# A decode kernel whose query weights arrive in another order: the last 128 rows of w_q first, in four loads over two queues, into a V buffer that is still free

## The chip, the cores and the metric

The kernel runs on one core of one Trainium2 chip. The metric is the device time in microseconds (us), lower is better. The kernel before takes 203.89 us (median of 3 runs, 203.78 to 204.10).

Engines are named as the profile names them: PE is TensorE's matmul, PEld its weight load, DVE is VectorE, ACT is ScalarE, POOL is GpSimd, and SP is SyncE, which here only issues DMAs. A DMA is issued on the queue of the engine that issues it (q1 is SP's, q10 is ACT's) and is carried by 16 DMA engines.

## The reference, cut to what matters

One token goes through an attention block with a cache of 4096 positions and then a gated feed-forward block. All tensors are bf16.

```python
# x [1,1,640]; k_cache, v_cache [1,32,4096,128]; wq [640,4096]; wo [4096,640]
# w_gate, w_up [640,1728]; w_down [1728,640]
q = layernorm(x) @ wq                              # 32 heads of 128
scores = einsum("bhqd,bhkd->bhqk", q, k) * 128**-0.5
o = einsum("bhqk,bhkd->bhqd", softmax(scores), v)
h = x + o @ wo
n = layernorm(h)
out = h + (gelu(n @ w_gate) * (n @ w_up)) @ w_down
```

K and V are 32 MB each, w_q and w_o 5 MB each, the three feed-forward weights 2.1 MB each.

## The kernel before, in words

**Groups.** The 32 heads are worked in 8 groups of 4 (`HG`, `NG`). A group's K is one 4096 KB load into one of two buffers `kbuf`, its V one load into one of two buffers `vbuf`; a partition holds 128 positions of one head, 32 partitions make a head.

**Query.** `query(g)` (L314) makes the queries of one group: five matmuls (L318), one per chunk of 128 rows of w_q, with the normalised x repeated over 128 columns (`xb`) as the stationary operand, so that every partition gets the query; four ACT copies (L324) then put each head's part into `qb`. `wq_sb` lies in `arena`, 5 rows of w_q (40 KB) in each partition; the same arena later takes `wo_sb`. All queries go through one PSUM tile, `pq`.

**Scores.** DVE multiplies K with `qb` in four pieces a group (`mult`, L339, into three `prod` buffers), PE adds up over the 128 columns with matmuls by the identity (`fold`, L359 and L350), DVE reduces the rest (`red`, L366). `top`, `turn`, `head` and `soft` find the maximum and make the exponentials `P4` on ACT (L395). The last `mult` of a group frees its K buffer (`kfree`).

**Values.** PE multiplies P with V (`values`, L406), 32 matmuls a group in four parts; the last frees the V buffer (`vfree`). `extract`, `column`, `total`, `spread`, `gather` and `place` bring the result into the column form that `project` (L612, w_o) needs. The last group's values go another way (`values_last`, L414).

**Behind the attention.** Layernorm of h, `up` (L659) for w_gate and w_up, the gelu on 14 columns, `down` (L697) with w_down, a copy and the store.

**Order.** The order is written out by hand: each engine runs its instructions in the order in which the calls to `S.op` and `S.dma` stand, and `Sched` adds semaphore waits where a call names a token. All loads but x are on SP's queue, in program order, so an issue that waits holds up those behind it: w_q (L247), K0, K1 (L257), V0 (L266); then at the end of each step n of the main loop the next V and K, K with a wait for `kfree`, V with a wait for `vfree` (V1 has none). `load_wo` waits for the last query (`t_qlast`), since w_o takes w_q's place. x (L278) is on ACT's queue. In the main loop queries 0 and 1 stand ahead of step 0, and query n+1 stands in step n for n from 1.

**Start.** While w_q arrives, DVE and POOL make constants, PE turns x into columns (L302: five matmuls of one row), and `layernorm` (L281) makes `xb` (L297).

## Time and profile before

| | |
|---|---|
| median of 3 runs | 203.89 us |
| the profiled execution | 203.82 us |
| its span, first to last instruction | 202.6 us |
| PE busy | 153.4 us (76%) |
| DVE busy | 116.1 us (57%) |
| ACT busy | 30.5 us (15%) |
| POOL busy | 2.4 us (1%) |
| bytes read from HBM | 84.23 MB, 416 GB/s over the span |
| w_q, issue to landing | 15.3 us |
| K loads, issue to landing, median | 25.1 us |
| V loads, issue to landing, median | 23.2 us |

Spans and windows count from the span's start. "DMA share" is the mean busy share of the 16 DMA engines; in a short window it can be above 1, because a packet is counted, with its whole duration, where it starts. A wait is put down to what the profile saw end last. The chain of waits is followed back from the last instruction, at each step to what released it.

### The profile page before, as it was taken

The page shows a single profiled execution, that of the slowest core. Times are in us where ns is not written, and L with a number is a line of the kernel's source. Part 1 is how long each engine was busy: PE and PEld are TensorE (multiplying, and loading weights), DVE is VectorE, ACT ScalarE, POOL GpSimd, SP SyncE. Part 2 cuts the span into 40 slices and gives each one's busy share as a digit, 9 for nine tenths or more (in the row PEclk, how much of TensorE's full clock was granted, in tenths as well). Part 3 has the DMA queues.
Part 4 walks back from the last instruction along what each step waited for, and adds up shares of the span by engine and source line. Part 5 has one row for each costly group of instructions (what it writes and reads, how often), then busy time and mean ns, then how long its engine had stood idle before and what let it go on. Part 6 is the DMA issues. An engine that isn't in the chain of part 4 may idle for free.

```text
span 202.6 us, 2291 instructions
## 1 busy us (share of the span) xinstructions
PE 153.4 (76%) x1084; PEld 49.8 (25%) x860; DVE 116.1 (57%) x153; ACT 30.5 (15%) x110; POOL 2.4 (1%) x8
## 2 busy tenths in 40 slices
PE   1005348689969957999899399959777999977775
PEld 1001000002211220322122113212100244666572
DVE  6200087998199518883993499269999513301121
ACT  2002200006004200150060006000604004000000
POOL 1000000000000000000000000000000000200000
PEclk9999999999999996999999999999999999975555
DMA  7999999999999999999999999999999999989992
GB/s 251 412 469 414 414 434 453 459 414 414 421 450 427 459 409 414 440 429 440 443 421 414 434 440 440 434 427 411 440 427 446 385 427 457 450 382 438 423 396 102
DMA packets 3939, 84.37 MB, mean 416 GB/s; under 512 B 441, under 2 KB 570, under 8 KB 986
## 3 DMA queue, kind: packets, MB, share of 16 engines
q1 hardware_dynamic: 3928, 84.23, 97.4%
q8 instruction: 7, 0.11, 0.2%
q14 instruction: 2, 0.02, 0.0%
q10 hardware_dynamic: 2, 0.00, 0.0%
HBM read 84.23 MB, written 0.00 MB: 416 GB/s over the span
## 4 chain that ended last, share of the span: by engine, by line
DMA 60%; DVE 28%; PE 10%; issue 1%; SPq 0%; DVEq 0%
DMA kbuf<-in_A_k_cache_dram 47%; DVE prod L339 19%; DMA wu_sb<-in_B_w_up_dram 13%; DVE sc L366 4%; PE pu L406 4%; PE pf L350 3%; DVE xz L424 2%; PE pu L659 1%; DVE xm L421 1%; PE pf L697 1%; PE pf L359 1%; DVE mx L374 1%; DVE mrow L383 0%; SPq L247 0%; DVE o_sb L701 0%
## 5 line engine op out<-in xcount | busy, mean ns | idle before, releaser
L339 DVE TENSOR_TENSOR prod<-kbuf,qb 128x4096 bf16<-128x4096 bf16 x32 | 72.8, 2278 | 46.4 <-DMA kbuf<-in_A_k_cache_dram 46.4
L350 PE MATMUL pf<-prod,Ibf 128*128 128x512 bf16 x224 | 57.0, 397 | 0.0
L359 PE MATMUL pf<-prod,Ibf 128*128 128x512 bf16 x32 | 13.1, 410 | 24.9 <-DVE prod L339 24.9
L406 PE MATMUL pg<-vbuf,P 128*16 128x512 bf16 x128 | 29.9, 379 | 0.0
L366 DVE TENSOR_REDUCE sc<-pf 128x32 f32<-128x512 f32 x32 | 21.6, 676 | 4.2 <-PE pf L350 4.2
L406 PE MATMUL pu<-vbuf,P 128*16 128x512 bf16 x96 | 22.2, 379 | 0.0
L318 PE MATMUL pq<-wq_sb,xb 128*128 128x512 bf16 x40 | 12.1, 442 | 12.5 <-DMA wq_sb<-in_A_wq_dram 11.3
L391 ACT ACTIVATE nb<-pm 128x4 f32<-128x4 f32 x8 | 1.4, 173 | 118.6 <-PE pm L388 118.6
L395 ACT ACTIVATE P<-sc,nb 32x128 bf16<-32x128 f32 x32 | 18.5, 577 | 0.9
L406 PEld LDWEIGHTS pg<-vbuf,P 128*16 128x16 bf16 x128 | 10.6, 90 | 20.0 <-issue 5.2
L359 PEld LDWEIGHTS pf<-prod,Ibf 128*128 128x128 bf16 x32 | 3.2, 99 | 45.5 <-DVE prod L339 40.5
L406 PEld LDWEIGHTS pu<-vbuf,P 128*16 128x16 bf16 x96 | 8.1, 90 | 16.9 <-issue 6.9
L324 ACT CAST qb<-pq 32x128 bf16<-32x128 f32 x32 | 8.2, 256 | 16.0 <-PE pq L318 15.2
L318 PEld LDWEIGHTS pq<-wq_sb,xb 128*128 128x128 bf16 x40 | 3.8, 111 | 17.3 <-issue 13.0
L612 PE MATMUL pf<-aP,wo_sb 128*128 128x32 bf16 x160 | 7.1, 194 | 1.2 <-issue 1.0
L395 ACT ACTIVATION_READ_ACCUMULATOR P<-sc,nb 32x1 f32 x32 | 8.0, 250 | 0.0
L424 DVE TENSOR_REDUCE xz<-xm 16x128 f32<-16x512 f32 x7 | 7.3, 1040 | 0.2
L612 PEld LDWEIGHTS pf<-aP,wo_sb 128*128 128x128 bf16 x160 | 6.8, 131 | 1.9 <-issue 1.5
L388 PEld LDWEIGHTS pm<-mrow,ones 1*128 1x128 f32 x16 | 2.3, 183 | 12.6 <-issue 10.9
L414 PE MATMUL pq<-P,vbuf 128*128 128x32 bf16 x128 | 3.6, 188 | 1.4 <-DMA vbuf<-in_A_v_cache_dram 1.4
L421 DVE TENSOR_TENSOR xm<-pg,rmask 16x512 f32<-16x512 f32 x4 | 2.7, 672 | 3.4 <-PE pg L406 3.4
L429 PEld LDWEIGHTS po<-hsel,xz 16*128 16x128 f32 x14 | 2.0, 183 | 10.1 <-DVE xz L424 9.7
(85 smaller groups left out, 58.1 us busy)
## 6 DMA issues: line engine op xcount, KB each, us to landing
kbuf<-in_A_k_cache_dram SPq DMA_DIRECT2D x8, 4096.0 KB, 25.1
vbuf<-in_A_v_cache_dram SPq DMA_DIRECT2D x8, 4096.0 KB, 23.2
wq_sb<-in_A_wq_dram SPq DMA_DIRECT2D x1, 5120.0 KB, 15.3
wo_sb<-in_A_wo_dram SPq DMA_DIRECT2D x1, 3840.0 KB, 28.7
wg_sb<-in_B_w_gate_dram SPq DMA_DIRECT2D x1, 2160.0 KB, 22.6
wu_sb<-in_B_w_up_dram SPq DMA_DIRECT2D x1, 2160.0 KB, 27.3
wo_sb<-in_A_wo_dram SPq DMA_DIRECT2D x1, 1280.0 KB, 17.8
wd_sb<-in_B_w_down_dram SPq DMA_DIRECT2D x1, 800.0 KB, 16.0
```

The costliest lines, as they stand in the source:

```text
L318: tok = S.op("tensor", lambda t, c=c, n0=n0: t.matmul(pq[:, :], xb[:, c, :], wq_sb[:, c, n0:n0 + HG * DH], start=(c == 0), stop=(c == NC_D ...
L324: t_qb[g] = S.op("scalar", lambda a, lo=lo, hi=hi, hh=hh: a.copy(qb[lo:hi, g, :], pq[lo:hi, hh * DH:(hh + 1) * DH]), [tok])
L339: return S.op("vector", lambda v: v.tensor_tensor(out=prod[n % NPR][:, :, :], in0=kbuf[g % 2][:, s * RP:(s + 1) * RP, :], in1=qb[:, g, :]. ...
L350: return t.add_instruction(m)
L359: return t.matmul(dst, Ibf[:, :], src, start=True, stop=False)
L366: red_done[n] = S.op("vector", lambda v: v.reduce_sum(sc[g % 2][:, s * RP:(s + 1) * RP], pf[n % 2][:, :].rearrange("p (r w) -> p r w", r=R ...
L395: t_exp[g] = S.op("scalar", lambda a, lo=lo, hi=hi, h=h, hh=hh: a.activation(P4[g % 2][lo:hi, :, hh], sc[g % 2][lo:hi, :], ACTF.Exp, bias= ...
L406: t_pv[g] = S.op("tensor", lambda t, i=i, r=r, last=last: t.matmul(pv[g % 2][0:VM, :], P4[g % 2][:, r:r + VR, :], vbuf[g % 2][:, r:r + VR, :],
L414: t_pv[g] = S.op("tensor", lambda t, r=r: t.matmul(pq[:, 0:WIDE], vbuf[g % 2][:, r, :], P4[g % 2][:, r, :].unsqueeze(1).to_broadcast([128, ...
L421: a = S.op("vector", lambda v: v.tensor_tensor(out=xm[:, :, :], in0=pv[g % 2][0:VM, :].rearrange("p (r d) -> p r d", r=VR), in1=rmask[:, : ...
L424: t_ext[g] = S.op("vector", lambda v: v.reduce_sum(xz[g % 2][:, :], xm[:, :, :].rearrange("p r d -> p d r"), axis=AX.X), [a, t_acc[g - 2] ...
L612: tok = S.op("tensor", lambda t, c=c, cc=cc, first=first, last=last: t.matmul(pp[:, cc * WIDE:(cc + 1) * WIDE], wo_sb[:, w, c, cc::NC_D], ...
```

## The change

w_q is split. Its first 512 rows still go into the arena, now 4 rows (32 KB) in each partition. Its last 128 rows go into `vbuf[1]`, the V buffer that is not used until V1 arrives: two rows (16 KB) in each of the partitions 32 to 95, in four loads of 16 partitions each (every fourth partition), two on SP's queue ahead of everything and two on ACT's queue behind x. The 64 other partitions of that tile are filled with zeros by POOL and DVE, and the matching entries of x are zero (`xr`), so that a chunk is again a matmul over 128 partitions; there are two such chunks. A query is six matmuls now, the two of the last rows first.

Because V1 needs the buffer, its load now waits for the last query (`t_qlast`), and it stands on SP's queue one step later, still between K2 and K3. All queries are made early: 0 to 4 ahead of the loop, 5 in step 0, 6 at the end of step 0, 7 in step 1. They alternate between the PSUM tiles `po` and `pq`; `column`, which writes `po` later, waits for the last query there. `x_sb` and `xr` lie in `xm`'s place.

```diff
@@ -15,6 +15,10 @@
 SK = 4096
 DF = 1728
 NC_D = D // 128
+NQM = 4
+NQN = 2
+NQC = NQM + NQN
+QM = 128 * NQM
 EPS = 1e-5
 SCALE = 1.0 / math.sqrt(DH)
 GELU_C0 = math.sqrt(2.0 / math.pi)
@@ -138,7 +142,8 @@
     def over(name, base, shape):
         return nc.alloc_sbuf_tensor_at(name, shape, BF16, offset=nc.lookup_mloc(base).addr)
 
-    wq_sb = over("wq_sb", arena, [128, NC_D, H * DH])
+    wq_sb = over("wq_sb", arena, [128, NQM, H * DH])
+    wq_n = over("wq_n", vbuf[1], [128, NQN, H * DH])
     wo_sb = over("wo_sb", arena, [128, NW, HW, D])
     wg_sb = over("wg_sb", kbuf[NG % 2], [128, NC_D, DF])
     wu_sb = over("wu_sb", kbuf[(NG + 1) % 2], [128, NC_D, DF])
@@ -165,13 +170,15 @@
     csel = sb("csel", [128, HW], BF16)
     jred = sb("jred", [128, DJ], FP32)
     cred = sb("cred", [128, HW], FP32)
-    x_sb = sb("x_sb", [1, D], BF16)
+    x_sb = over("x_sb", xm, [1, D])
+    xr = nc.alloc_sbuf_tensor_at("xr", [1, NQN, 128], BF16, offset=nc.lookup_mloc(xm).addr + 2 * D)
     x32 = sb("x32", [128, NC_D], FP32)
+    xq = sb("xq", [128, NQC], FP32)
     h32 = sb("h32", [128, NC_D], FP32)
     sq = sb("sq", [128, NC_D], FP32)
     st = sb("st", [128, 4], FP32)
     ln = sb("ln", [128, 8], FP32)
-    xb = sb("xb", [128, NC_D, 128], BF16)
+    xb = sb("xb", [128, NQC, 128], BF16)
     hln = sb("hln", [128, NC_D], BF16)
     g_t = sb("g_t", [128, NF], FP32)
     t1 = sb("t1", [128, NF], FP32)
@@ -206,6 +213,7 @@
     pv = [pg, pu]
 
 
+    t_xr = S.op("vector", lambda v: v.memset(xr[:, :, :], 0.0))
     t_one = S.op("vector", lambda v: v.memset(ones[:, :], 1.0))
     t_part = S.op("vector", lambda v: v.memset(part[:, :], 1.0 / D))
     S.op("vector", lambda v: v.memset(eps[:, :], EPS))
@@ -218,6 +226,7 @@
     t_ibf = S.op("gpsimd", lambda g: g.affine_select(
         Ibf[:, :], ones_bf[:, :], pattern=[[1, 128]], compare_op=ALU.is_equal,
         fill=0.0, base=0, channel_multiplier=-1), [t_onebf])
+    t_n0 = S.op("gpsimd", lambda g: g.memset(wq_n[0:32, :, :], 0.0))
 
     t_e4 = S.op("vector", lambda v: v.reduce_sum(
         e4[:, :], I32[:, :].rearrange("p (j i) -> p j i", j=4), axis=AX.X), [t_i32])
@@ -244,8 +253,16 @@
     t_cs = S.op("vector", lambda v: v.tensor_copy(csel[:, :], cred[:, :]), [b])
 
 
-    d_wq = S.dma("sync", "wq", lambda s: s.dma_start(
-        wq_sb[:, :, :], A_wq[:, :].rearrange("(p c) n -> p c n", c=NC_D)))
+    def load_q(eng, j):
+        return S.dma(eng, "wqn" + eng, lambda s: s.dma_start(
+            wq_n[32 + j:96:4, :, :],
+            A_wq[QM + 32 * j:QM + 32 * (j + 1), :].rearrange("(i t) n -> i t n", t=NQN)))
+
+    d_wqn = []
+    for j in range(2):
+        d_wqn.append(load_q("sync", j))
+    d_wqm = S.dma("sync", "wq", lambda s: s.dma_start(
+        wq_sb[:, :, :], A_wq[0:QM, :].rearrange("(p c) n -> p c n", c=NQM)))
 
     def cache(src, g):
         return src[0, g * HG:(g + 1) * HG, :, :].rearrange("h (q r) d -> (h q) r d", r=R)
@@ -265,10 +282,11 @@
             lo, hi = cuts[i], cuts[i + 1]
             tok = S.dma("sync", "v%d_%d" % (g % 2, i), lambda s, lo=lo, hi=hi: s.dma_start(
                 vbuf[g % 2][:, lo:hi, :], cache(A_v_cache, g)[:, lo:hi, :]),
-                [vfree[g - 2] if g >= 2 else None])
+                [vfree[g - 2] if g >= 2 else t_qlast])
             d_v[g] += [tok] * (hi - lo)
 
 
+    t_qlast = None
     load_k(0)
     load_k(1)
     load_v(0)
@@ -277,6 +295,8 @@
     S.op("scalar", lambda a: a.preload_act_table_set("natural_log_exp_and_others"), token=False)
     d_x = S.dma("scalar", "x", lambda a: a.dma_start(
         x_sb[:, :], A_x[0, :, :]))
+    for j in range(2, 4):
+        d_wqn.append(load_q("scalar", j))
 
     def layernorm(src, t_src, o, dst, ps, beside=None):
         b = S.op("vector", lambda v: v.scalar_tensor_tensor(
@@ -297,32 +317,46 @@
         return S.op("vector", lambda v: v.tensor_scalar(
             dst[0], dst[1], ps[:, 0:1], ln[:, q + 2:q + 3], ALU.subtract, ALU.mult), [f])
 
+    t_xr = S.op("vector", lambda v: v.tensor_copy(
+        xr[:, :, 32:96].rearrange("o t (i j) -> o t i j", j=4),
+        x_sb[:, QM:D].rearrange("o (j i t) -> o t i j", j=4, t=NQN)), [d_x, t_xr])
     a = None
-    for c in range(NC_D):
-        a = S.op("tensor", lambda t, c=c: t.matmul(
-            pm[:, c:c + 1], x_sb[0:1, c::NC_D], ones_bf[0:1, 0:1],
-            start=(c == 0), stop=(c == NC_D - 1), skip_group_check=True),
-            [d_x, t_onebf], token=(c == NC_D - 1))
+    rows = [x_sb[0:1, c::NC_D] for c in range(NC_D)]
+    rows += [x_sb[0:1, c:QM:NQM] for c in range(NQM)]
+    rows += [xr[0:1, t, :] for t in range(NQN)]
+    for c, row in enumerate(rows):
+        last = c == len(rows) - 1
+        a = S.op("tensor", lambda t, c=c, row=row, last=last: t.matmul(
+            pm[:, c:c + 1], row, ones_bf[0:1, 0:1],
+            start=(c == 0), stop=last, skip_group_check=True),
+            [d_x, t_onebf, t_xr if c >= NC_D + NQM else None], token=last)
+    S.op("vector", lambda v: v.tensor_copy(xq[:, :], pm[:, NC_D:NC_D + NQC]), [a])
     t_x32 = S.op("vector", lambda v: v.tensor_copy(x32[:, :], pm[:, 0:NC_D]), [a])
     t_x32 = S.op("vector", lambda v: v.reduce_sum(st[:, 0:1], x32[:, :], axis=AX.X), [t_x32])
     t_xb = layernorm(x32, t_x32, 0, (
-        xb[:, :, :], x32[:, :].unsqueeze(2).to_broadcast([128, NC_D, 128])), pz)
+        xb[:, :, :], xq[:, :].unsqueeze(2).to_broadcast([128, NQC, 128])), pz)
+    t_n1 = S.op("vector", lambda v: v.memset(wq_n[96:128, :, :], 0.0))
 
 
     t_qb = [None] * NG
+
+    last_wqn = list(dict(d_wqn).items())
 
     def query(g):
         tok = None
-        for c in range(NC_D):
-            n0 = g * HG * DH
-            tok = S.op("tensor", lambda t, c=c, n0=n0: t.matmul(
-                pq[:, :], xb[:, c, :], wq_sb[:, c, n0:n0 + HG * DH],
-                start=(c == 0), stop=(c == NC_D - 1)),
-                [t_xb, d_wq, t_qb[g - 1] if g else None], token=(c == NC_D - 1))
+        ps = pq if g % 2 else po
+        n0 = g * HG * DH
+        for i in range(NQC):
+            c = (i + NQM) % NQC
+            w = wq_sb[:, c, n0:n0 + HG * DH] if c < NQM else wq_n[:, c - NQM, n0:n0 + HG * DH]
+            waits = [d_wqm] if c < NQM else [t_n0, t_n1] + last_wqn
+            tok = S.op("tensor", lambda t, c=c, w=w, i=i: t.matmul(
+                ps[:, :], xb[:, c, :], w, start=(i == 0), stop=(i == NQC - 1)),
+                [t_xb, t_qb[g - 2] if g >= 2 else None] + waits, token=(i == NQC - 1))
         for hh in range(HG):
             lo, hi = hh * PPH, (hh + 1) * PPH
             t_qb[g] = S.op("scalar", lambda a, lo=lo, hi=hi, hh=hh: a.copy(
-                qb[lo:hi, g, :], pq[lo:hi, hh * DH:(hh + 1) * DH]), [tok])
+                qb[lo:hi, g, :], ps[lo:hi, hh * DH:(hh + 1) * DH]), [tok])
         return tok
 
 
@@ -332,7 +366,6 @@
     t_rz, t_aP = [None] * NW, [None] * NW
     t_zz, t_aL = [None], [None]
     n_piece = 0
-    t_qlast = None
 
     def mult(g, s):
         n = g * NP + s
@@ -427,7 +460,8 @@
 
     def column(g):
         t_acc[g] = S.op("tensor", lambda t: t.matmul(
-            po[:, g * HG:(g + 1) * HG], xz[g % 2][:, :], hsel[:, :], start=True, stop=True), [t_ext[g]])
+            po[:, g * HG:(g + 1) * HG], xz[g % 2][:, :], hsel[:, :], start=True, stop=True),
+            [t_ext[g], t_qb[NG - 2]])
 
     def total(w):
         t_zz[0] = S.op("tensor", lambda t: t.matmul(
@@ -457,8 +491,8 @@
 
     CH = NV // 4
 
-    query(0)
-    query(1)
+    for g in range(NG - 3):
+        query(g)
     t_mul = {}
     t_g = None
     for n in range(NG - 1):
@@ -487,8 +521,10 @@
             soft(p)
         if w is not None:
             total(w)
-        if 2 <= n + 1 < NG:
-            t_qlast = query(n + 1)
+        if n == 0:
+            query(NG - 3)
+        if n == 1:
+            t_qlast = query(NG - 1)
         fold(n, 2, t_mul[2])
         red(n, 1)
         if w is not None:
@@ -513,7 +549,10 @@
 
         if n == 0:
             load_k(2)
+            query(NG - 2)
+        elif n == 1:
             load_v(1)
+            load_k(3)
         elif n == NG - 3:
             load_k(n + 2)
             load_v(n)
```

`NG` is 8, so `range(NG - 3)` is queries 0 to 4. On SP's queue two issues more stand ahead of the 512 rows; behind them the order K0, K1, V0, K2, V1, K3, ... is the same as before. On PE the queries of steps 2 to 6 are gone from there.

## The prediction

> **What bounds the kernel now.** I read the page's slices first, then the table of queues, then the chain that ended last.
>
> ```profile
> DMA  7999999999999999999999999999999999989992
> GB/s 251 412 469 414 414 434 453 459 414 414 421 450 427 459 409 414 440 429 440 443 421 414 434 440 440 434 427 411 440 427 446 385 427 457 450 382 438 423 396 102
> ...
> q1 hardware_dynamic: 3928, 84.23, 97.4%
> ...
> DMA kbuf<-in_A_k_cache_dram 47%; DVE prod L339 19%; DMA wu_sb<-in_B_w_up_dram 13%; DVE sc L366 4%; PE pu L406 4%; PE pf L350 3%; DVE xz L424 2%; PE pu L659 1%; DVE xm L421 1%; PE pf L697 1%; PE pf L359 1%; DVE mx L374 1%; DVE mrow L383 0%; SPq L247 0%; DVE o_sb L701 0%
> ```
>
> From the second slice to the 39th the 16 DMA engines are busy nine tenths or more (one slice shows 8); SP's queue q1 carries 84.23 MB and its packets take 97.4% of 16 engines' span. The chain gives 60% of the span to DMA. So the span is start of the flow + 84.23 MB at the queue's rate + a tail behind the last loads. The chain in order of time shows both ends (start us, us, what):
>
> ```profile
> 1.24 24.57 DMA kbuf<-in_A_k_cache_dram
> ...
> 167.75 27.28 DMA wu_sb<-in_B_w_up_dram
> 195.04 0.04 issue
> 195.08 2.55 PE pu L659 x70
> ```
>
> The chain begins with K, whose load lies behind w_q's on the queue, and near the end `wu_sb` lands at 195.04, after which only 7.6 us of compute and the store are left (202.6). TensorE had been ready before that, as the timeline says:
>
> ```profile
> 195.08 2.53 PE L659 MATMUL pu<-hln,wu_sb 128*128 128x32 bf16 x70 [1.17 <-DMA wu_sb<-in_B_w_up_dram]
> ```
>
> It stood idle 1.17 us for `wu_sb`. So if the whole stream comes earlier by some tenths, the end does too, up to 1.17 us; beyond that the attention's last column is late next.
>
> Since the bytes are the same in both kernels, all depends on the start. The windows of 0.25 us count a packet where it starts. Columns: window, its length, PE, PEld, DVE, ACT, POOL busy, PEclk, DMA share, GB/s.
>
> ```profile
> 1.50:1.75 0.25, 0.00 (x0) 0.00 (x0) 0.25 (x2) 0.25 (x1) 0.22 (x1) 1.00 0.01 5
> 1.75:2.00 0.25, 0.00 (x0) 0.00 (x0) 0.25 (x3) 0.25 (x1) 0.00 (x0) 1.00 7.15 1966
> 2.00:2.25 0.25, 0.13 (x3) 0.14 (x4) 0.25 (x3) 0.08 (x1) 0.00 (x0) 1.00 1.28 328
> 2.25:2.50 0.25, 0.22 (x5) 0.13 (x4) 0.14 (x2) 0.00 (x0) 0.00 (x0) 1.00 0.50 164
> 2.50:2.75 0.25, 0.00 (x0) 0.00 (x0) 0.25 (x3) 0.00 (x0) 0.00 (x0) 1.00 0.39 164
> 2.75:3.75 1.00, 0.00 (x0) 0.00 (x0) 1.00 (x8) 0.00 (x0) 0.00 (x0) 1.00 0.00 0
> 3.75:4.00 0.25, 0.00 (x0) 0.00 (x0) 0.22 (x3) 0.00 (x0) 0.00 (x0) 1.00 0.76 328
> 4.00:4.25 0.25, 0.00 (x0) 0.00 (x0) 0.21 (x3) 0.00 (x0) 0.00 (x0) 1.00 1.89 819
> 4.25:4.50 0.25, 0.14 (x1) 0.14 (x1) 0.05 (x2) 0.00 (x0) 0.00 (x0) 1.00 2.27 983
> 4.50:4.75 0.25, 0.25 (x2) 0.25 (x2) 0.00 (x0) 0.00 (x0) 0.00 (x0) 1.00 0.76 328
> 4.75:5.00 0.25, 0.20 (x1) 0.11 (x1) 0.02 (x1) 0.00 (x0) 0.00 (x0) 1.00 0.00 0
> 5.00:5.25 0.25, 0.00 (x0) 0.00 (x0) 0.21 (x1) 0.01 (x1) 0.00 (x0) 1.00 0.38 164
> ```
>
> A w_q row of one partition is 40 KB (40,960 B), one packet, so GB/s x window / 40,960 B is the number of packets that start there, and share x 16 x window their durations. 1.50 holds x's 1.25 KB. Then 12 packets start in 1.75 to 2.00 and take 7.15 x 16 x 0.25 = 28.6 us together, 2.38 each; 2 of 2.56; one of 2.0; and the last, which starts after 2.50, 1.56. That is one first packet on each of 16 engines, mean (28.6 + 5.1 + 2.0 + 1.6) / 16 = 2.33 us. The second packets (2, 5, 6, 2, and a straggler after 5.00) take 0.76 x 4 / 2 = 1.52 each, and so do all later ones. **So each engine loses 2.33 - 1.52 = 0.8 us on its first packet.** The row that matters is that of 2.50: the engine served last loses nothing. The delay is not a charge on every first packet; something common lets the flow go at about 2.6 us, when the last engine has got its first row.
>
> **The change, part by part.**
>
> *Start of the stream.* Removed: one load of 128 x 40 KB. Added: four of 16 x 16 KB (two on SP's queue, two on ACT's behind x) and one of 128 x 32 KB; 5 x 1024 KB either way. At one end the gain is nothing (a loss is the third case below). At the other end the flow would begin as x's did: x's packet starts in 1.50 to 1.75 (middle 1.63) and w_q's on average at 1.98, which adds 0.35 to the 0.8: 1.15 us at most. I take 0.6, half of it, nearer the row of 2.50: a load of 16 rows has every engine served after an eighth of 128 rows, and the next small load is there 0.44 us later (SP's issues start at 0.81, 1.24 and 1.70), while 256 KB last 0.6 us at 430 GB/s. What keeps me from the full 1.15 is that no row shows a 16-row load start on an idle queue.
>
> x took 1.29 us from issue (0.82) to the matmul that waited for it (2.11). w_q's landing 15.3 us after issue is 3.2 us more than its bytes need (K's 4096 KB behind it land 25.81 - 16.11 = 9.7 us later, 5/4 of that is 12.1). [...]
>
> *Packets.* Each engine gets 4 packets of 16 KB and 8 of 32 KB for 8 of 40 KB, and 4 more of the short ones that end a load. In 20 to 160 us (32 KB packets) the windows give 430 GB/s at a share of 1.00; in 193 to 197 (6 KB and less) 402 at 0.98, that is 410. 1 MB at 410 instead of 430 is 2.56 - 2.44 = 0.12 us. This is the upper end, 0 the lower; I take +0.1.
>
> *Small work at the start.* Six more matmuls of x (five take 0.35 us), a memset and copy for `xr` and one for `xq` (0.16 us rows like L306), xb with 768 columns for 640 (0.94 us becomes 1.13): under 1.2 us. POOL clears 32 x 8192 (its row at L588, 1280 columns in 1.16 us, makes 7.4 us, done at 9.1); DVE clears another 32 (256 words in 0.28 us make some 4.4 us, done near 12). All of it is hidden by TensorE's 11.3 us wait for w_q, which ends at 16.25; without that cover it would cost 5 to 10 us. The early rows give no early query: each query also needs the 512 rows, last of w_q to land.
>
> *Queries.* 8 x 6 matmuls for 8 x 5. Five queries now stand ahead of the first fold: 28 matmuls behind the landing, at 0.43 us (from start to start in the first query, five in 2.29) 12 us, so 16.25 + 12 = 28.3, against 28.19 where fold waits for DVE's first product anyway; at the later 0.25 us each they end by 24. ACT's 1.1 us of copies per query alternate over two PSUM tiles. Queries 5, 6 and 7 add 18 - 5 = 13 matmuls, 3.3 us, to TensorE in 28 to 47, where it stood idle 0.65 + 0.90 + 0.90 + 0.91 us between folds. DVE, which frees K, waits for a fold by at most some tenths. From the third group on TensorE and ACT have 1.25 and 1.1 us less per group, off the path: 0.
>
> *The new wait.* V1 shares its buffer with w_q's last rows, so its load waits for query 7; behind it on SP stands K3. Starts, as before had them:
>
> ```profile
> 37.53 0.33 SPq L257 DMA_DIRECT2D kbuf<-in_A_k_cache_dram  x1
> ...
> 37.91 0.43 SPq L266 DMA_DIRECT2D vbuf<-in_A_v_cache_dram  x1
> ...
> 45.63 1.25 PE L318 MATMUL pq<-wq_sb,xb 128*128 128x512 bf16 x5
> ```
>
> K2 is issued at 37.53 and lands at 54.97; V1 went right behind it. Query 7 stands where query 2's 1.25 us stood at 45.63, so V1 goes out near 47 to 48.5, and K3, which had waited for DVE until 49.24, close to where it was. The queue has K2 to carry until 54.97. With x's 1.29 us from issue to landing, V1 could go as late as 53.7: cover of 5 us. Cost 0; if the cover went, each us later would cost one. wo's wait for the last query (3.0 us of SP at 143) goes; V6 is in the queue ahead of it, so nothing comes of it.
>
> *Sum.* -0.6 + 0.1 = -0.5 us. Against the profiled execution: 203.82 (span 202.6 and 1.22 around it) - 0.5 = 203.3. It stands 0.07 under the median 203.89, so as a median **203.4 us**. A measurement of this kernel can tell some 0.2% (0.4 us) from no change.
>
> **The rivals.**
>
> *The start costs what it did* (0.27). If the common event is not the handing out of rows but something that comes 0.8 us after the first read whatever is read, only the packets' +0.1 is left: 204.0. For it: 14 engines start within half a microsecond and yet wait until about 2.6 us. Against it: x was read and landed by 2.11.
>
> *The small loads stutter, slower* (0.12). Each load that reaches an engine only when the one before is done could pay the first packet's 0.8 us anew. Place: SP's second small load and its 512 rows; 2 x 0.8 = 1.6, half of it covered by ACT's packets: +0.8, and +0.1: 204.8. It decides once rows reach an engine over 0.6 us after the load before. For: the issues leave 0.6 - 0.44 = 0.16 us only, and no load of before was issued just in time. Against: the second queue's 512 KB add 1.2 us of cover. [...]
>
> *V1 too late* (0.03): TensorE over 5 us behind in group 1; 1 us late gives 205.
>
> **The numbers.** Forecast 0.58, its own range -1.1 to -0.2 (202.8 to 203.7), four fifths of it beyond -0.4. Faster 0.58 x 0.8 = 0.46; same 0.12 + 0.27 = 0.39; slower 0.12 + 0.03 = 0.15. The range 202.8 to 204.2 leaves out the slower cases and a little at the low end.
>
> **What would show it.** Right: in the 0.25 us windows the first 16 KB packets take well under 1.4 us (0.6 for the bytes and 0.8), the engines reach 1.0 share before 2.6, K0 lands before 25.5, `wu_sb` lands near 194.5. Second case: 16 KB packets of about 1.4 us and K0 at 25.9. Stutter: windows with a share below 1 between 3 and 5 us. V1 too late: a gap in the DMA slices at 55 us. Wrong in any case if a stall of DVE on `qb` or of TensorE on `wq_n` shows behind K0's landing.

## The result, and the profile after

The changed kernel takes 206.14 us (median of 11 runs; before 203.89, median of 11 on the same chip). The ratio of the mean times is 1.0086, interval 1.0057 to 1.0115: slower by 0.9%, where 203.4 and a range of 202.8 to 204.2 were forecast. One of the 11 executions, the profiled one, took 369.56 us, with TensorE far slower throughout (busy for 348 us instead of 156); it is left out of the ratio, and the profile shown here is that of a second measurement of the same kernel (first experiment below).

That profiled execution took 205.76 us, span 204.5, against 203.82 and 202.6. Its slices and queues answer to the first lines of the prediction:

```profile
DMA  6999999999999999999999999999999999999992
GB/s 186 391 410 436 436 442 429 423 436 436 436 410 442 429 442 429 417 436 426 449 423 429 429 423 461 410 426 429 436 449 410 406 415 461 439 392 434 421 390 78
...
q1 hardware_dynamic: 3992, 83.71, 95.8%
q10 hardware_dynamic: 66, 0.53, 1.1%
...
DMA 59%; DVE 22%; PE 16%; SPq 1%; issue 0%; DVEq 0%
```

The stream still bounds the kernel, and the loss is in the first three slices: 186, 391 and 410 GB/s for 251, 412 and 469, together 145 GB/s less over slices of 5.1 us, 0.74 MB, which is 1.7 us at 430 GB/s (part of it only a matter of which packets have already started; counted by what was carried, 1.4 us, below). Behind them both kernels run alike (431 and 430 GB/s from 20 to 160 us). The chain in order of time (start us, us, what) begins with issues now:

```profile
0.81 0.61 SPq L257
1.42 0.06 issue
1.48 0.57 SPq L257
2.09 0.75 SPq L264
2.88 24.22 DMA kbuf<-in_A_k_cache_dram
27.13 2.30 DVE prod L372
...
169.83 27.17 DMA wu_sb<-in_B_w_up_dram
197.04 2.53 PE pu L698 x70
```

SP's two small loads take 0.61 and 0.57 us to issue, the 512 rows 0.75, and K0 goes out at 2.88 for 1.24. K0 lands for DVE at 27.13 for 25.84, 1.29 us later, and `wu_sb` at 197.04 for 195.08, 1.96 later: all that the profiled execution lost (1.94 us). TensorE's wait for `wu_sb` grew from 1.17 to 1.98 us, so 0.81 of the 1.96; the other 1.15 us are that TensorE itself was ready for it that much later:

```profile
197.04 2.52 PE L698 MATMUL pu<-hln,wu_sb 128*128 128x32 bf16 x70 [1.98 <-DMA wu_sb<-in_B_w_up_dram]
```

**Where the first slice lost it.** The windows of a quarter of a microsecond at the start. As in the prediction, GB/s x window / packet size is the number of packets that start in a row, and share x 16 x window their durations; a small load's packet is 16 KB (16,384 B), which takes 0.61 us at an engine's share of 430 GB/s.

```profile
2.00:2.25 0.25, 0.04 (x1) 0.05 (x2) 0.25 (x4) 0.09 (x1) 0.25 (x1) 1.00 1.03 262
2.25:2.50 0.25, 0.25 (x8) 0.25 (x9) 0.20 (x2) 0.00 (x0) 0.25 (x1) 1.00 2.77 721
2.50:2.75 0.25, 0.19 (x6) 0.11 (x4) 0.20 (x2) 0.00 (x0) 0.25 (x1) 1.00 0.25 66
2.75:3.00 0.25, 0.00 (x0) 0.00 (x0) 0.25 (x3) 0.00 (x0) 0.25 (x1) 1.00 0.00 0
3.00:3.25 0.25, 0.00 (x0) 0.00 (x0) 0.25 (x6) 0.00 (x0) 0.25 (x1) 1.00 0.16 66
3.25:3.50 0.25, 0.00 (x0) 0.00 (x0) 0.25 (x6) 0.00 (x0) 0.25 (x1) 1.00 2.26 918
3.50:3.75 0.25, 0.00 (x0) 0.00 (x0) 0.25 (x6) 0.00 (x0) 0.25 (x1) 1.00 0.17 66
3.75:4.00 0.25, 0.00 (x0) 0.00 (x0) 0.25 (x6) 0.00 (x0) 0.25 (x1) 1.00 1.44 590
4.00:4.25 0.25, 0.00 (x0) 0.00 (x0) 0.25 (x6) 0.00 (x0) 0.25 (x1) 1.00 1.43 459
4.25:4.50 0.25, 0.00 (x0) 0.00 (x0) 0.25 (x6) 0.00 (x0) 0.25 (x1) 1.00 0.30 66
4.50:4.75 0.25, 0.00 (x0) 0.00 (x0) 0.25 (x6) 0.00 (x0) 0.25 (x1) 1.00 2.45 328
4.75:5.00 0.25, 0.00 (x0) 0.00 (x0) 0.25 (x6) 0.00 (x0) 0.25 (x1) 1.00 0.49 66
5.00:5.25 0.25, 0.00 (x0) 0.00 (x0) 0.25 (x6) 0.00 (x0) 0.25 (x1) 1.00 1.47 328
5.25:5.50 0.25, 0.00 (x0) 0.00 (x0) 0.25 (x6) 0.00 (x0) 0.25 (x1) 1.00 1.59 262
...
4.25:7.00 2.75, 0.00 (x0) 0.00 (x0) 2.75 (x6) 0.00 (x0) 2.75 (x1) 1.00 0.92 238
```

From 2.00 to 2.75 there are 4 + 11 + 1 = 16 packets, as many as there are engines, of (1.03 + 2.77 + 0.25) x 4 / 16 = 1.0 us: the first small load, 0.4 us over its bytes' time, where before's first 16 packets were 0.8 over theirs. They start at 2.33 us on average (middles of the windows), before's in the prediction's rows at 1.98. The next 16 start from 3.00 to 3.75 and take 0.65; the third 16 from 3.75 to 4.25, at 0.72. So three loads of 256 KB went out in 2.25 us, 0.75 each, where their bytes need 0.61. Little is lost up to here, because before's first packets were held longer. Then it gets worse: the five packets of the row of 4.50 take 2.45 x 4 / 5 = 2.0 us, and the 16 that start from 4.25 to 5.50 take (0.30 + 2.45 + 0.49 + 1.47 + 1.59) x 4 / 16 = 1.58 us each, 0.97 over their bytes' time. The row over the whole stretch in which the fourth small load and the 512 rows begin, from 4.25 to 7.00, has 238 GB/s at a share of 0.92. At 430 that would have been 2.75 x (1 - 238 / 430) = 1.23 us shorter: K0's 1.29 us, nearly.

A share near 1 with 238 GB/s says that the engines were not simply empty. The trace also keeps the start, duration, size and queue of every packet, though not its engine. By these records the four groups of 16 are SP's first small load, ACT's first, SP's second and ACT's second. In flight (begun and not ended) are about 16 packets from 2.75 to 4.25 us, 14.4 on average from 4.25 to 4.75, 10.8 from 4.75 to 5.25 and about 16 from then on. If an engine carries one at a time, the gap is worth (1.6 + 5.2) x 0.5 / 16 = 0.2 us, an estimate. Most of the loss came while as many packets were in flight as there are engines, in packets that ran slow. Six of ACT's second load, the slow ones of 4.25 to 4.75, began within 0.01 us of the end of an earlier packet, so they were not late; why they ran slow is not shown.

### The profile page after: what moved, and what is told of

It reads as the page before. It is cut to its first block, busy times and chain, and to the rows that moved or that the text cites. A ratio compares the mean times of both kernels' runs of the same rounds, so it can differ in the third digit from the quotient of the medians.

```text
span 368.3 us, 2323 instructions
## 1 busy us (share of the span) xinstructions
PE 348.3 (95%) x1098; PEld 73.3 (20%) x874; DVE 127.4 (35%) x157; ACT 30.5 (8%) x110; POOL 9.3 (3%) x9
## 4 chain that ended last, share of the span: by engine, by line
PE 94%; DVE 4%; issue 1%; ACT 0%; DVEq 0%
PE pf L383 36%; PE pg L439 21%; PE pu L439 15%; PE pf L392 5%; PE po L353 4%; PE pq L353 4%; PE pf L651 2%; DVE hrow L237 2%; PE pq L447 1%; PE pm L421 1%; PE pm L411 1%; PE po L462 1%; DVE wq_n L338 1%; PE pg L698 1%; PE pf L736 1%; PE pu L698 1%
## 5 line engine op out<-in xcount | busy, mean ns | idle before, releaser
L383 PE MATMUL pf<-prod,Ibf 128*128 128x512 bf16 x224 | 140.4, 829 | 0.0
L439 PE MATMUL pg<-vbuf,P 128*16 128x512 bf16 x128 | 77.1, 808 | 0.0
L439 PE MATMUL pu<-vbuf,P 128*16 128x512 bf16 x96 | 57.8, 814 | 0.0
L439 PEld LDWEIGHTS pg<-vbuf,P 128*16 128x16 bf16 x128 | 17.6, 144 | 61.7 <-issue 61.5
L439 PEld LDWEIGHTS pu<-vbuf,P 128*16 128x16 bf16 x96 | 14.1, 151 | 51.4 <-issue 51.3
L416 DVE TENSOR_REDUCE mrow<-pm 1x4 f32<-1x128 f32 x8 | 2.2, 279 | 61.1 <-PE pm L411 61.1
L392 PE MATMUL pf<-prod,Ibf 128*128 128x512 bf16 x32 | 20.3, 633 | 0.0
L353 PE MATMUL po<-wq_n,xb 128*128 128x512 bf16 x8 | 5.6, 836 | 6.1 <-DVE wq_n L338 6.1
L353 PE MATMUL po<-wq_sb,xb 128*128 128x512 bf16 x16 | 10.5, 836 | 0.0
L353 PE MATMUL pq<-wq_sb,xb 128*128 128x512 bf16 x16 | 10.5, 836 | 0.0
L462 PEld LDWEIGHTS po<-hsel,xz 16*128 16x128 f32 x14 | 3.5, 295 | 24.1 <-DVE prod L372 23.0
```

Of the source, the lines that this page charges most:

```text
L353: tok = S.op("tensor", lambda t, c=c, w=w, i=i: t.matmul(ps[:, :], xb[:, c, :], w, start=(i == 0), stop=(i == NQC - 1)), [t_xb, t_qb[g - 2 ...
L383: return t.add_instruction(m)
L392: return t.matmul(dst, Ibf[:, :], src, start=True, stop=False)
L439: t_pv[g] = S.op("tensor", lambda t, i=i, r=r, last=last: t.matmul(pv[g % 2][0:VM, :], P4[g % 2][:, r:r + VR, :], vbuf[g % 2][:, r:r + VR, :],
```

## The experiments

The theory after the first look: **several small loads in a row at the head of idle queues cost more to hand out than their bytes take**, so the stream falls behind before the large loads carry it. The rivals: the early queries or V1's new wait; the use of two queues; the form of the loads (every fourth partition); and extra work for the 16 KB packets wherever they stand.

Two numbers per kernel help to sort them, both of the profiled execution. One is the mean GB/s of the packets that start from 1.75 to 8.25 us; 6.5 us at 403 GB/s is 2.62 MB, what before has started by then. A packet counts there with all its bytes, so what is in flight at 8.25 us (0.18 to 0.37 MB by the packet records) blurs it by up to some 30 GB/s. The last column is free of that: the MB carried by 20 us, from the packet records, a packet in flight counted by the share of its time that has passed. The changed kernel is 0.62 MB behind there, 1.4 us at 430 GB/s.

| kernel | loads ahead of the large w_q load | GB/s, 1.75 to 8.25 | first product of K0, us | `wu_sb` used, us | ratio to before (interval) | MB carried by 20 us |
|---|---|---|---|---|---|---|
| before | none | 403 | 25.84 | 195.08 | 1 | 7.45 |
| early queries only | none | 403 | 25.84 | 194.91 | 1.0007 (0.9985 to 1.0030) | 7.44 |
| small loads last | none (four behind) | 403 | 25.41 | 195.56 | 1.0005 (0.9993 to 1.0017) | 7.44 |
| one of 64 partitions | 1 x 1 MB | 398 | 25.68 | 195.28 | 1.0015 (0.9999 to 1.0031) | 7.35 |
| two of 64 partitions | 2 x 512 KB | 403 | 25.38 | 195.31 | 1.0025 (1.0012 to 1.0037) | 7.35 |
| half first | 2 x 256 KB | 383 | 26.33 | 197.90 | 1.0051 (1.0023 to 1.0079) | 7.29 |
| four of 64 partitions | 4 x 256 KB | 318 | 26.92 | 196.84 | 1.0124 (1.0097 to 1.0152) | 6.94 |
| changed | 4 x 256 KB | 303 | 27.13 | 197.04 | 1.0103 (1.0074 to 1.0131) | 6.83 |
| all four on SP | 4 x 256 KB | 308 | 27.94 | 197.22 | 1.0130 (1.0101 to 1.0159) | 6.65 |
| two of 32 partitions | 2 x 512 KB | 292 | 28.29 | 197.32 | 1.0134 (1.0092 to 1.0176) | 6.45 |
| four of neighbours | 4 x 256 KB | 202 | 31.25 | 201.06 | 1.0323 (1.0295 to 1.0352) | 4.91 |

In the fourth and fifth columns are starts in the profiled execution; in "half first" and "four of 64 partitions" K0's first product waited last for `qb`, not for K0. The last column follows the ratio but for neighbours in the table whose intervals overlap.

### The changed kernel again

No edit.

> The changed kernel once more, for a profile of an undisturbed execution. Hand-out theory (the five loads at the start are handed to the DMA engines later than the engines empty them): some 205.7 us, with w_q's last part and K0 landing 1.1 to 1.4 us later than before (K0 near 26.9 instead of 25.8), and a stretch between 4.7 and 5.5 us from the span's start in which few packets start. Rival, the early queries and V1's wait: K0 lands at 25.8 as before and the time is lost later, as DMA share below 1 somewhere after 50 us.

Measured: 206.37 us, 1.0103 (1.0074 to 1.0131). Its profile is the one above. The loss is there again, of the same size within the intervals.

### Only the early queries and V1's wait

Before's single w_q load of five rows a partition, with the new order of queries (the alternating PSUM tiles and the wait in `column`, also in this edit, are left out here):

```diff
-                [vfree[g - 2] if g >= 2 else None])
+                [vfree[g - 2] if g >= 2 else t_qlast])
...
-    query(0)
-    query(1)
+    for g in range(NG - 3):
+        query(g)
...
         if n == 0:
             load_k(2)
+            query(NG - 2)
+        elif n == 1:
             load_v(1)
+            load_k(3)
```

> Only half of the change: w_q comes in one load as before, but all queries are made early, alternate between po and pq, and V1 waits for the last query. Hand-out theory: like before, 203.7 to 204.1. Rival, early queries and V1's wait: all or most of the loss stays, 205 or more.

Measured: 203.92 us, 1.0007 (0.9985 to 1.0030); K0 at 25.84 as before. Queries, V1's wait and the earlier `wo` issue cost nothing that can be measured. So what is lost comes with the split of w_q: its loads, or the clears and the sixth matmul that go with them.

### All four small loads on SP's queue

```diff
-    for j in range(2):
+    for j in range(4):
         d_wqn.append(load_q("sync", j))
...
-    for j in range(2, 4):
-        d_wqn.append(load_q("scalar", j))
```

> The changed kernel with all four small loads on SP's queue. An issue of such a load took about 0.6 us. Hand-out theory: SP spends 2.6 us on four issues, so the 512 rows go out 1.2 us later still, K0 lands at 27.5 or later and the time is 206 to 207. Rival, two queues on one DMA engine disturb each other: with one queue the loss goes, 203.9 to 204.3.

Measured: 206.49 us, 1.0130 (1.0101 to 1.0159), beside 206.37 for two queues on the same chip. SP's own timeline of this kernel:

```profile
0.81 2.50 SPq L257 DMA_DIRECT2D wq_n<-in_A_wq_dram  x4
3.35 0.58 SPq L264 DMA_DIRECT2D wq_sb<-in_A_wq_dram  x1
```

The four take 2.50 us to issue, 0.63 each; the 512 rows leave SP only at 3.93 (2.84 in the changed kernel), and K0 is later still (27.94). So a loss of this size needs no second queue. But it is made up differently: by the packet records this kernel has 11.6 packets in flight on average from 4.25 to 6.75 us, for 14.6 in the changed one, and its small loads' packets take 0.64, 0.72, 0.82 and 0.67 us on average, none the 1.58 of ACT's second load. Here the engines did run short. The second queue hides SP's issue time, but the interval leaves no gain of it in the total.

### The small loads behind the 512 rows

```diff
     d_wqn = []
-    for j in range(2):
-        d_wqn.append(load_q("sync", j))
     d_wqm = S.dma("sync", "wq", lambda s: s.dma_start(
         wq_sb[:, :, :], A_wq[0:QM, :].rearrange("(p c) n -> p c n", c=NQM)))
+    for j in range(4):
+        d_wqn.append(load_q("sync", j))
...
-    for j in range(2, 4):
-        d_wqn.append(load_q("scalar", j))
```

> The changed kernel with the 512 rows first and the four small loads behind them on SP's queue. Hand-out theory: the small loads are handed out while the engines have 512 rows to carry, so the start is that of before, K0 lands at 25.9 and the time is 203.8 to 204.2. Rival, the 16 KB packets or their partitions are slow by themselves: the loss stays wherever they stand, 205 or more.

Measured: 204.12 us, 1.0005 (0.9993 to 1.0017). The row of 1.75 to 8.25 us (columns as above; the last is GB/s):

```profile
1.75:8.25 6.50, 0.49 (x9) 0.41 (x9) 6.39 (x12) 0.34 (x1) 6.50 (x2) 1.00 1.05 403
```

The same four loads, as many packets, the same clears and the same queries: no loss. This is the run that places the cost: it is their position at the head, ahead of the large load. With the run before it, which has them all on SP's queue too, it clears the queue as well. It clears the 16 KB packets, the sixth matmul of a query and POOL's work too.

### Four loads of 16 neighbouring partitions

```diff
-            wq_n[32 + j:96:4, :, :],
+            wq_n[32 + 16 * j:48 + 16 * j, :, :],
...
-        xr[:, :, 32:96].rearrange("o t (i j) -> o t i j", j=4),
-        x_sb[:, QM:D].rearrange("o (j i t) -> o t i j", j=4, t=NQN)), [d_x, t_xr])
+        xr[:, :, 32:96],
+        x_sb[:, QM:D].rearrange("o (i t) -> o t i", t=NQN)), [d_x, t_xr])
```

> The changed kernel with each small load into 16 neighbouring partitions instead of every fourth one; four loads, two queues and sizes as they are. Theory A, the step of four partitions makes the issue and the hand-out long (0.6 us against 0.38 to 0.45 of a 128-partition load): issues fall to some 0.4 us, the 512 rows go out 0.6 us earlier, K0 lands near 26.4 instead of 27.1, the time is 204.6 to 205.4. Theory B, every load costs a hand-out of its own whatever its partitions: issues stay at 0.6 us and the time at 205.5 to 206.5.

Measured: 211.0 us, 1.0323 (1.0295 to 1.0352). The issues are shorter (SP's two take 0.85 us together for 1.23), so a step of four between partitions does lengthen an issue. But the packets are much slower:

```profile
4.75:5.25 0.50, 0.00 (x0) 0.00 (x0) 0.50 (x6) 0.00 (x0) 0.50 (x1) 1.00 2.24 262
```

8 packets of 16 KB, 2.24 x 16 x 0.5 / 8 = 2.24 us each, where the changed kernel's second load, at a step of four, takes 0.65. From 4.25 to 7.00 us the profile has 95 GB/s at a share of 0.82, for 238 at 0.92 in the changed kernel. This swamps what the run was to test. It shows that 16 neighbours were a worse choice here than every fourth partition (1.0323 for 1.0103); why their packets run slower is not shown.

### One load of 64 neighbouring partitions

```diff
-            wq_n[32 + j:96:4, :, :],
-            A_wq[QM + 32 * j:QM + 32 * (j + 1), :].rearrange("(i t) n -> i t n", t=NQN)))
+            wq_n[32:96, :, :],
+            A_wq[QM:D, :].rearrange("(i t) n -> i t n", t=NQN)))
...
-    for j in range(2):
-        d_wqn.append(load_q("sync", j))
+    d_wqn.append(load_q("sync", 0))
...
-    for j in range(2, 4):
-        d_wqn.append(load_q("scalar", j))
```

> The changed kernel with the last 128 rows as one load into the 64 neighbouring partitions, on SP's queue ahead of the 512 rows; ACT's queue carries x alone. Hand-out theory: 1 MB in one hand-out lasts the engines 2.4 us, longer than the next load needs to arrive, so no hole: K0 lands at 25.7 to 26.1, 203.8 to 204.4. Rival, anything that stands ahead of the 512 rows or fills few partitions costs: K0 at 26.5 or later, 205 or more.

(x's copy into `xr` follows the rows to their new partitions, here and in all later edits of this kind.) Measured: 204.27 us, 1.0015 (0.9999 to 1.0031), K0 at 25.68. The same megabyte at the head in one load instead of four costs nothing that is certain.

### Before, with w_q in two loads of all 128 partitions

The first row of every partition (8 KB) in a load of its own, the other four (32 KB) behind it:

```diff
+    d_wq = [S.dma("sync", "wq%d" % lo, lambda s, lo=lo, hi=hi: s.dma_start(
+        wq_sb[:, lo:hi, :], A_wq[:, :].rearrange("(p c) n -> p c n", c=NC_D)[:, lo:hi, :]))
+        for lo, hi in ((0, 1), (1, NC_D))]
```

> The kernel before with w_q in two loads over 128 partitions: one row (8 KB) of each partition first, then the other four (32 KB). If the first packet's 0.8 us are bytes at a slow rate, 8 KB packets pay a fifth of it and K0 lands at 25.2, 203.3. If the flow is held until the hand-out of the first load is over, whatever its packets' size, K0 lands at 25.7 to 25.9 and the time is 203.8 to 204.0.

Measured: 203.85 us, 1.0001 (0.9987 to 1.0014). K0 is used at 25.14, 0.7 us earlier than before, and yet nothing is won:

```profile
1.75:2.00 0.25, 0.00 (x0) 0.00 (x0) 0.25 (x3) 0.25 (x1) 0.00 (x0) 1.00 1.79 295
```

Nine packets of 8 KB (8,192 B) start here and take 1.79 x 4 / 9 = 0.80 us, where their bytes need 0.30. That is 0.5 us too long, for 0.86 in before's row (2.38 for 1.52). So smaller first packets are held less. But as many bytes have started by 8.25 us as in before (403 GB/s), and by 20 us it has carried 7.52 MB for 7.45, 0.16 us ahead, which is hardly more than chance (7.49 in the next kernel, whose total is that of before). The total's interval, -0.3 to +0.3 us, can't resolve that. K0's landing is no measure of the stream: it came 0.7 us earlier although the stream as a whole gained so little.

### Before, with x's load 1.1 us later

```diff
     d_x = S.dma("scalar", "x", lambda a: a.dma_start(
-        x_sb[:, :], A_x[0, :, :]))
+        x_sb[:, :], A_x[0, :, :]), [t_rs])
```

> The kernel before with x's load (ACT's queue) issued 1.1 us later, behind a wait for a memset of DVE. If two queues share one hand-out, w_q's rows reach the engines earlier without x beside them: first packets start before 1.75, K0 lands at 25.5 or earlier, 203.5 to 203.7. If not: 25.8 and 203.9 as before.

Measured: 203.77 us, 0.9998 (0.9987 to 1.0009), K0 at 25.78. x's small load beside w_q neither holds the flow nor costs anything that can be measured.

### Two loads of 32 partitions

```diff
-            wq_n[32 + j:96:4, :, :],
-            A_wq[QM + 32 * j:QM + 32 * (j + 1), :].rearrange("(i t) n -> i t n", t=NQN)))
+            wq_n[32 + j:96:2, :, :],
+            A_wq[QM + 64 * j:QM + 64 * (j + 1), :].rearrange("(i t) n -> i t n", t=NQN)))
...
-    for j in range(2):
+    for j in range(1):
...
-    for j in range(2, 4):
+    for j in range(1, 2):
```

> The changed kernel with two loads of 32 partitions (every second one) instead of four of 16: one on SP's queue, one on ACT's behind x; the bytes and the 16 KB rows stay. If a small load costs its hand-out once, some 0.8 us whatever its rows, then 512 KB last the engines 1.2 us, the 512 rows arrive in time, and nearly all of the loss goes: K0 near 25.9, 203.9 to 204.4. If the hand-out goes with the rows, the hole stays: K0 at 26.8 or later, 205.5 or more.

Measured: 207.21 us, 1.0134 (1.0092 to 1.0176), K0 at 28.29. As a test of the number of loads this run is inconclusive, because the packets changed too:

```profile
2.75:3.25 0.50, 0.00 (x0) 0.00 (x0) 0.50 (x6) 0.00 (x0) 0.50 (x1) 1.00 2.06 492
```

15 packets of 2.06 x 8 / 15 = 1.10 us. By the packet records the first 16 take 0.71 us, the other 48 from 1.04 to 1.13 (means of 16), together 1.5 us over their bytes' time (the means added up). The first 32 packets of the 512 rows behind them, into all 128 partitions, are slow too: 1.90 and 1.70 us for the 1.22 of their bytes. So the step of two is not the whole reason.

### Two small loads ahead, two behind

```diff
-    for j in range(2):
+    for j in range(1):
         d_wqn.append(load_q("sync", j))
     d_wqm = S.dma("sync", "wq", lambda s: s.dma_start(
         wq_sb[:, :, :], A_wq[0:QM, :].rearrange("(p c) n -> p c n", c=NQM)))
+    for j in (1, 3):
+        d_wqn.append(load_q("sync", j))
...
-    for j in range(2, 4):
+    for j in range(2, 3):
```

> The changed kernel with two small loads ahead (one on SP's queue, one on ACT's) and the other two behind the 512 rows on SP's. If each small load ahead of the 512 rows costs about a third of a microsecond (a quarter of the 1.3 by which K0 is late), half of them leave about half of it: K0 near 26.5, 204.4 to 205.1. If the loss is one of having any small load at the head or two queues at all, it stays whole: K0 at 27.1, 205.5 to 206.5.

Measured: 205.22 us (203.87 to 206.61), 1.0051 (1.0023 to 1.0079): half of the loss with half of the loads ahead. The profiled execution was the slowest one; its `wu_sb` (197.90) has a second cause in it, since V7 was issued at 170.64 (166.43 in before) and the queue ran short around 170 to 172 (266 GB/s). Its start is not touched by that: 383 GB/s, between 403 and 303, and 7.29 MB by 20 us, a quarter of what the changed kernel is behind.

### Four loads of 64 partitions, and two

To tell the number of loads from the form of 16 partitions, each load now takes 64 neighbouring partitions: four of 256 KB (4 KB a partition), or two of 512 KB (8 KB a partition), on the same two queues.

```diff
-            wq_n[32 + j:96:4, :, :],
-            A_wq[QM + 32 * j:QM + 32 * (j + 1), :].rearrange("(i t) n -> i t n", t=NQN)))
+            wq_n[32:96, j // 2, (j % 2) * 2048:(j % 2) * 2048 + 2048],
+            A_wq[QM:D, :].rearrange("(i t) n -> i t n", t=NQN)[:, j // 2, (j % 2) * 2048:(j % 2) * 2048 + 2048]))
```

> The changed kernel with the same number of small loads of the same 256 KB on the same queues, but each over 64 neighbouring partitions (half a row, 4 KB, in each) instead of 16 at a step of four. If the number of loads ahead of the 512 rows is what costs (each a hand-out longer than its 0.6 us of data), the loss stays: K0 lands at 26.7 to 27.3, 205 to 206.5. If the cost lies in the shape of 16 rows at a step, it goes: K0 at 25.9, 204.0 to 204.4, as with one load of 64 partitions.

```diff
-            wq_n[32 + j:96:4, :, :],
-            A_wq[QM + 32 * j:QM + 32 * (j + 1), :].rearrange("(i t) n -> i t n", t=NQN)))
+            wq_n[32:96, j, :],
+            A_wq[QM:D, :].rearrange("(i t) n -> i t n", t=NQN)[:, j, :]))
...
-    for j in range(2):
+    for j in range(1):
...
-    for j in range(2, 4):
+    for j in range(1, 2):
```

> The changed kernel with two small loads of 512 KB over 64 neighbouring partitions (one row, 8 KB, in each), one on SP's queue and one on ACT's. If a load costs a hand-out of some 0.8 us, two times 1.2 us of data cover three hand-outs and the loss nearly goes: K0 at 25.8 to 26.1, 204.0 to 204.5. If two queues at the start are what costs, a loss stays: K0 at 26.4 or later, 204.8 or more.

Measured: four loads 206.11 us, 1.0124 (1.0097 to 1.0152); two loads 204.04 us, 1.0025 (1.0012 to 1.0037). Their rows, four loads first:

```profile
1.75:8.25 6.50, 0.49 (x9) 0.41 (x9) 6.39 (x12) 0.34 (x1) 6.50 (x2) 1.00 0.92 318
```

```profile
1.75:8.25 6.50, 0.49 (x9) 0.41 (x9) 6.39 (x12) 0.34 (x1) 6.50 (x2) 1.00 1.03 403
```

The same partitions and bytes ahead, on the same queues: four loads lose what the changed kernel loses, two lose a fifth of it. (Their packets are 4 KB and 8 KB, so this pair alone doesn't separate number from packet size; but the changed kernel, with 16 KB packets, lost as much as the four of 4 KB.) So between these kernels it is the number of loads and the little that each brings. A load of 256 KB is 0.61 us of bytes, one of 512 KB 1.22, and SP's issues are some 0.65 us apart. By the packet records the kernel with four has 14.6 packets in flight on average from 3.25 to 6.25 us, the one with two 16. If an engine carries one at a time, that difference is worth only some 0.3 us, 1.4 x 3 / 16, an estimate, of the 1.2 by which the first is behind at 20 us, so here too most was lost in packets that ran slow. Of the theory, then, the place and the number of the loads stand; that it is the handing out that takes longer is not shown.

None of these kernels measurably beats the one before.

**What stays open.** First, why packets run slow behind several small loads, and what part the later issue of the large load has in it: its issue ended at 1.19 us in before, at 2.02 to 2.08 with one small load ahead on SP's queue, at 2.84 or 2.85 with two (2.13 with neighbours) and at 3.93 with four. The three at 2.04 to 2.08 with full-rate packets have 383, 398 and 403 GB/s, and by the bytes at 20 us they are 0.2 to 0.4 us behind, so the later issue alone does little up to there; beyond it no run varied one without the other. Second, `wu_sb` is 1.96 us late and K0 only 1.29, though the DMA share is 1.00 from 20 to 160 us in both kernels. The windows at the end narrow it down. Changed kernel (the next to last column is the DMA share):

```profile
198.00:199.00 1.00, 1.00 (x36) 1.00 (x33) 0.00 (x0) 0.00 (x0) 0.00 (x0) 0.50 1.03 407
199.00:200.00 1.00, 0.67 (x26) 0.56 (x26) 0.30 (x2) 0.00 (x0) 0.00 (x0) 0.50 0.77 301
200.00:201.00 1.00, 1.00 (x31) 0.71 (x27) 0.15 (x2) 0.00 (x0) 0.00 (x0) 0.50 0.47 177
201.00:202.00 1.00, 1.00 (x36) 0.45 (x24) 0.04 (x1) 0.00 (x0) 0.00 (x0) 0.50 0.07 24
```

Before:

```profile
198.00:199.00 1.00, 1.00 (x29) 0.72 (x33) 0.15 (x2) 0.00 (x0) 0.00 (x0) 0.50 0.71 269
199.00:200.00 1.00, 1.00 (x32) 0.47 (x28) 0.10 (x1) 0.00 (x0) 0.00 (x0) 0.50 0.20 72
```

Adding up the shares, the engines end on average at 199 + 0.77 + 0.47 + 0.07 = 200.31 us and at 198 + 0.71 + 0.20 = 198.91: 1.40 us apart, about what the start lost (1.4 us by the bytes at 20 us). The rest, 0.56 us of the 1.96, would then be that the engines end further apart, if a load is there only when its last engine is done. Which engine lags, and whether since the start, isn't shown. Third, the median lost some tenths more than the profiled execution (206.37 - 203.99 = 2.4 for 1.94); the kernels with early queries issue V7 later than before's 166.43 us (167.79 in the one with only them, 168.50 in the changed one), and in the profiled run of the half-first kernel, at 170.64, the queue ran short. That it explains the tenths was not tested.

## Why the prediction was wrong

**What bounds the kernel** was right: the stream does, TensorE waits for `wu_sb`, and what the start loses reaches the end.

**Start of the stream: here it failed.** The term was -0.6 us (bounds -1.15 to 0) and came out at about +1.3 at K0. Its reason was that a load of 16 rows has every engine served early and that "the next small load is there 0.44 us later", inside the 0.61 us that 256 KB last, so that the small loads follow one another at full rate. Neither held.

The engines were not served earlier: the first packets start at 2.33 us on average for 1.98. And SP issued at 0.81, 1.48 and 2.09, not at 0.81, 1.24 and 1.70: 0.67 and 0.61 us apart. The 0.44 came from loads of 128 partitions. Before's own timeline had a nearer row, the eight issues of `wd_sb`, loads of few and spaced partitions, 5.09 us together, 0.64 each:

```profile
175.89 5.09 SPq L592 DMA_DIRECT2D wd_sb<-in_B_w_down_dram  x8
```

With it the margin of 0.16 us is gone before anything is assumed of the engines. ACT's first load hid that at first: up to 4.25 us about 16 packets were in flight.

Nor did the packets run at full rate, and this is the largest part. Against before, roughly and in us, taking each group of 16 packets as one on each engine (an estimate, since the records do not name the engine): first packets later +0.35, held less -0.41 (0.40 for 0.81), second load +0.04, third +0.11, fourth (ACT's second) +0.97, the gap behind the third +0.2, the first packets of the 512 rows +0.12 (1.34 for 1.22 by the packet records). Together that is 1.4 us, what is missing in bytes by 20 us. How far the spacing of the issues is behind the slow fourth load is not shown.

The marks for "right" were half met, and that is worth noting: the first 16 KB packets did take well under 1.4 us, and the share passed 1.0 before 2.6. They say nothing of the loads behind the first.

Whether a start 0.6 us shorter would have been worth 0.6 us was not tested. Before with 8 KB first packets shortened their excess from 0.86 to 0.5 us and brought K0 0.7 us forward, but the whole stream gained 0.16 us at most, and the total stayed at 1.0001. So K0's landing, one of the marks, would have misled. The case "the start costs what it did", with 0.27, fits that kernel; in the changed one the start cost more.

**The stutter rival** came nearest, at 0.12: slower, and lost among the small loads. Its place was SP's second small load and the 512 rows, and its condition a load that reaches an engine only when the one before is done. What lost most was ACT's second small load, whose first six packets were not late and still took 1.83 us on average. Its mark, windows with a share below 1 between 3 and 5 us, decides nothing: before's own rows in the prediction have 0.00 from 2.75 to 3.75, since a packet is counted where it starts. Its price was 1.6 us "half of it covered by ACT's packets", +0.8. ACT's queue bought little: with all on SP the total is no different, and the slowest packets were ACT's own. The loss was 1.3 us at K0 and 1.9 to 2.4 at the end. From 1.75 to 8.25 us the changed kernel has 303 GB/s, for 403 in before; two loads of 512 KB on 64 neighbouring partitions have 403 as well, and cost a quarter of a per cent.

**Packets**, +0.1: in the kernel with the small loads last, which has all of them and no loss at the head, the total is 0.05% up with an interval of -0.07 to +0.17%, that is -0.15 to +0.35 us. Consistent, not resolved.

**Small work at the start**, 0: right in its cost, wrong in its times. DVE's timeline, changed kernel:

```profile
2.55 6.20 DVE L237 CAST hrow<-hx 128x32 bf16<-128x32 f32 x1
...
13.48 3.47 DVE L338 MEMSET wq_n<- 32x4096 uint32 x1 [0.91 <-issue]
```

The cast took 0.18 us in before. Now it lasts until 8.75, when POOL's clear of `wq_n` is over (1.79 to 8.70). So DVE's part of the clear is done at 16.95, not near 12, and the first query starts at 17.17 for 16.25. The 512 rows, issued at 2.09 and landed 15.3 us later by the page, came no sooner, and K0 came at 27.13: the cover was enough, with nothing to spare at the first query.

**Queries**, 0, and **V1's wait**, 0: nothing speaks against them. Early queries alone measure 1.0007 (0.9985 to 1.0030), which leaves room for up to 0.6 us. SP's timeline, changed kernel:

```profile
37.95 0.33 SPq L274 DMA_DIRECT2D kbuf<-in_A_k_cache_dram  x1
47.56 0.33 SPq L283 DMA_DIRECT2D vbuf<-in_A_v_cache_dram  x1
49.68 0.33 SPq L274 DMA_DIRECT2D kbuf<-in_A_k_cache_dram  x1
```

V1 goes out at 47.56, in the forecast 47 to 48.5, K3 at 49.68 for 49.24, and no slice near 55 us shows a gap.

## What to carry to other kernels

At the head of an idle stream, put the largest load first and the small ones behind it: four 256 KB loads ahead cost 0.9 to 1.3% here (3% where each went to 16 neighbouring partitions), the same four behind the large one nothing measurable, one or two larger loads ahead 0.15 to 0.25% on 64 neighbouring partitions (two on every second partition 1.3%). When a load is split, take the issue time from a row with the same partition pattern, and compare the spacing of the issues with the time that one piece's bytes last; if the margin is a few tenths, do not count on a gain. Judge a start by the bytes that the whole stream has moved some microseconds later, and not by the first tensor to land, which came 0.7 us earlier in one kernel whose stream gained 0.16.

## What the runs showed of the hardware that was not expected

- **Issue time goes with the pattern, but not only.** 16 partitions at a step of four took 0.55 to 0.64 us, 16 neighbours less (two in 0.85), 64 neighbours 0.58 to 0.64, 128 partitions 0.38 at the head of before. The 512 rows, also 128 partitions, took 0.42 to 0.75 behind small loads.
- **The rate of a small load went with the partitions it writes, but not only.** 16 KB packets take 2.24 us for 16 neighbours, 1.10 at a step of two, and 0.65 in the second load at a step of four. But the fourth load at a step of four took 1.58, and the single load of 64 neighbours 0.61 to 0.63 behind its first 16 packets (packet records), so the pattern alone does not decide.
- **The first packets mostly took longer than their bytes.** First packets of 40, 16 and 8 KB take 2.38, 1.0 and 0.80 us in the rows above, 0.86, 0.4 and 0.5 over their bytes' time; with x's load 1.1 us later the total is the same (0.9998). It is not always so: with all four small loads on SP's queue the first 16 KB packets took 0.64 us, with half of them first 0.67.
- **Work on DVE lasted as long as a clear on POOL.** A cast that takes 0.18 us in before took 6.20 in the changed kernel, from 2.55 to 8.75 us, and five reductions behind it 5.60 to 6.10; POOL's 6.91 us memset ran from 1.79 to 8.70. In six other kernels with this memset the cast took 6.19 or 6.20. Four DVE instructions that began beside the memset before 2.4 us took 0.09 to 0.24, so not every one was held; why these were is not shown.
